# Attention and a gated convolutional network on one core: the same jobs issued in another order

## The chip, the core and the metric

The kernel runs on one core of a Trainium2 chip. The core's engines each work through a queue of their own, in order: TensorE (PE in the profile; PEld is its weight load), VectorE (DVE), ScalarE (ACT), GpSimd (POOL) and SyncE (SP), which here only issues DMAs. Engines wait for one another through semaphores. The metric is the device time of one execution in microseconds (us); the number quoted for a kernel is the median of its runs.

## What is computed

Attention over 8 batches of 8 heads, with rotary positions, and behind it a feed-forward stage whose gate is a causal convolution of five taps:

```python
q_rot, k_rot = rotate(q), rotate(k)                 # q, k, v: 8 x 8 x 576 x 64
scores = np.matmul(q_rot, k_rot.transpose(0, 1, 3, 2)) / np.sqrt(64)
attn = np.exp(scores - scores.max(-1, keepdims=True))
attn = attn / (attn.sum(-1, keepdims=True) + 1e-09)
x = np.matmul(attn, v)          # heads side by side: 8 x 576 x 512
gate_pre = sum(conv_w[k] * xp[:, k:k + S] for k in range(5))   # xp: x with 4 zeros ahead
gate = 1 / (1 + np.exp(-gate_pre))
out = (gate * (x @ w_val)) @ w_out                  # w_val, w_out: 512 x 512
```

## The kernel before

The 64 heads are worked on as 32 pairs, two heads side by side on the 128 partitions; four pairs make a batch. For one pair, in the order of the data:

- q and k are loaded (`load`, line 300 and 304) and multiplied by the cosine and the sine table (`rope_mul`, line 312: two instructions for a piece). Pair 0's products are added up on PE by `rope_mm` (line 327), by one product with the identity and one with `swap`, a signed exchange of halves that ACT writes at the start (`make_swap`, line 760); the sum is then cast by ACT (`qk_hi`, line 339). Later pairs add on DVE or GpSimd (`rope_add`, line 318). The tables arrive as two DMAs of 288 columns each; `tab_wrap` (line 763) copies 128 columns of the second to the table's end, and the warm-up of ACT's table stands behind the second one's issue. `k_wrap` (line 362) repeats the head of k behind its tail.
- `s_mm` (line 392) and `s_mix` (line 402) compute the scores into PSUM in nine tiles of 128 by 576; for each, `s_max` (line 428, DVE) scales the tile into SBUF and takes the row's bound, and `s_exp` (line 436, ACT) takes the exponential and its sum. Eight of them are tiles of one head (`p` in the profile) and the ninth holds the rest of both heads (`pm`).
- `t_mm` (line 412) transposes the exponentials on PE, `t_copy` (line 505 on ACT, 507 on DVE) takes them out of PSUM, and `pv_mm` and `pv_left` (lines 518 and 528) multiply them by v.
- `r_add` (line 536, GpSimd) adds the small constant to the nine sums, `r_inv` (line 545, DVE) takes the reciprocal, which is written into nine spare columns behind `pm`. So the last transpose of the pair, of `pm` with 73 columns ("64*73" in the profile and "73x64" in the order), needs the reciprocal of that pair. From there the sums go through DRAM to `x_norm` (line 577, DVE).
- `tap` (lines 603 to 610; two instructions on GpSimd), `x_hi` and `x_lo` (lines 584 and 591) prepare the network; `f_mm` (line 636) multiplies a batch by a weight, split in a high and a low half, in eight parts of six products for each pair of halves; `y_mul`, `y_hi`, `y_lo` (lines 649 to 664) come between the two weights, and `o_out`, `o_dma` (lines 677 and 681) write the result.

The weights and the taps arrive as 64-bit numbers, which arithmetic on their two halves turns into 32 bit in eight steps for each quarter of a weight (`weight_step`, lines 694 to 720) and six for the taps (`tap_step`).

The order is a table written out by hand of 3087 jobs, `ORDER` (line 38). `Plan.run` walks through it and issues each job to its engine; a letter behind a number picks the engine where there is a choice (V for DVE, A for ACT, G for GpSimd), `:n` picks the buffer, and `a<b` lets a job on PE wait for another. Jobs with two-input forms that DVE and GpSimd share (`PAIRED`, among them `rope_mul`, `rope_add`, `tap`, `x_lo`, `y_lo` and `weight_step`) wait, where they stand on GpSimd, for the last such job that stands before them on DVE. So the table sets the rows of every engine's queue. `FILLS` puts 20 products of no use on PE before one entry of the table, at the start. For pairs 0 to 6 (`WHOLE`, line 37) q and k are held in one piece; from pair 7 on they are split in a high and a low half, which triples the score products.

## Time and profile before

| what | us |
|---|---|
| runs of the kernel | 620.59, 621.61, 622.41 |
| median | 621.61 |
| profiled execution, its own time | 620.63 |
| span of the profiled execution | 618.8 |
| PE busy in the span | 609.4 (98%) |
| DVE busy | 526.8 (85%) |
| ACT busy | 472.9 (76%) |
| GpSimd (POOL) busy | 328.6 (53%) |

The span runs from the first instruction to the end of the last transfer; the execution's own time is 1.83 us longer. Busy time is the time in which at least one instruction of the engine is under way. Instructions of one engine overlap a little: the next one often starts 0.08 us before the end of the one ahead. PE's products are pipelined, and one that waits for its operand inside the pipeline still counts as busy, so a busy PE can hide waits.

### The profile page before, as it was taken

How to read it: one execution, taken by the hardware profiler on the slowest of the kernel's cores; microseconds unless marked ns; L12 is line 12 of the kernel's file. 1: busy time of each engine (PE TensorE's matmuls, PEld its weight loads, DVE VectorE, ACT ScalarE, POOL GpSimd, SP SyncE). 2: the span in 40 equal slices, each digit the busy share in tenths (PEclk: the TensorE clock that was granted, in tenths of full speed). 3: DMA queues.
4: the chain of work that ended last, by engine and by line, in shares of the span. 5: the costliest groups of instructions: out<-in, count | busy, mean ns of one | idle time of the engine just before them, and what ended most of it. 6: DMA issues, size and time to landing. Idle time of an engine off the chain costs nothing.

```text
span 618.8 us, 21223 instructions
## 1 busy us (share of the span) xinstructions
PE 609.4 (98%) x8797; PEld 511.8 (83%) x8797; DVE 526.8 (85%) x1091; ACT 472.9 (76%) x993; POOL 328.6 (53%) x306
## 2 busy tenths in 40 slices
PE   8899999999999999999999999999999999999997
PEld 7566679888897979879898889788888889889697
DVE  6999999999998899998888888989888888777653
ACT  4999999999878887788887788766768775767421
POOL 2366444635445656466455457564454654688441
PEclk9999999999999999999999999999999999999999
DMA  8564631543524341435343234342333524201202
GB/s 252 171 200 149 197 115 58 155 138 119 158 68 147 100 137 64 139 118 158 117 140 119 81 119 137 116 140 64 96 119 100 177 62 149 90 20 52 71 21 77
DMA packets 42722, 72.85 MB, mean 118 GB/s; under 512 B 15449, under 2 KB 18050, under 8 KB 42626
## 3 DMA queue, kind: packets, MB, share of 16 engines
q1 hardware_dynamic: 41938, 70.74, 36.3%
q8 instruction: 69, 1.13, 0.8%
q10 hardware_dynamic: 688, 0.75, 0.4%
q14 instruction: 27, 0.22, 0.1%
HBM read 61.89 MB, written 9.59 MB: 115 GB/s over the span
## 4 chain that ended last, share of the span: by engine, by line
PE 88%; DVE 6%; DMA 2%; ACT 2%; issue 1%; SPq 0%; DVEq 0%; POOL 0%; POOLq 0%
PE ps_f L636 34%; PE ps_a L518 18%; PE ps_s L392 16%; PE ps_t L412 11%; PE ps_s L402 4%; PE ps_a L528 3%; DVE p L428 3%; ACT p L436 1%; ACT pt L505 1%; PE ps_s L412 1%; DMA wst<-in_w_val 1%; DVE qin L312 1%; DMA rb<-rd 1%; DMA tab<-in_tab 1%; DVE pm L428 0%
## 5 line engine op out<-in xcount | busy, mean ns | idle before, releaser
L436 ACT ACTIVATE p<-p,nm 128x576 f32<-128x576 f32 x256 | 197.3, 773 | 33.3 <-DVE p L428 32.1
L428 DVE TENSOR_SCALAR_CACHE_REDUCE p<-ps_s 128x576 f32<-128x576 f32 x256 | 184.1, 752 | 24.3 <-PE ps_s L392 21.4
L505 ACT COPY pt<-ps_t 128x1024 f32<-128x1024 f32 (+1 forms) x138 | 126.0, 929 | 23.8 <-PE ps_t L412 22.3
L392 PE MATMUL ps_s<-k,q 64*128 64x288 f32 x1424 | 137.5, 316 | 1.6 <-DVE q L318 0.5
L518 PE MATMUL ps_a<-pt,v 128*64 128x320 f32 (+1 forms) x1024 | 133.2, 410 | 0.1
L392 PEld LDWEIGHTS ps_s<-k,q 64*128 64x128 f32 x1424 | 111.5, 185 | 17.6 <-issue 4.0
L636 PE MATMUL ps_f<-y,wout_hi 64*128 64x288 f32 (+2 forms) x1024 | 109.0, 298 | 0.0
L518 PEld LDWEIGHTS ps_a<-pt,v 128*64 128x64 f32 x1024 | 69.9, 137 | 47.1 <-DVE p L428 1.1
L606 DVE SCALAR_TENSOR_TENSOR g<-x,cw,g 128x576 f32<-128x576 f32 (+2 forms) x113 | 93.3, 828 | 7.1 <-POOL g L604 3.6
L412 PEld LDWEIGHTS ps_t<-ident,p 64*128 64x128 f32 x2172 | 86.1, 139 | 10.3 <-issue 2.2
L412 PE MATMUL ps_t<-ident,p 64*128 64x64 f32 x2172 | 92.2, 223 | 0.4
L636 PEld LDWEIGHTS ps_f<-y,wout_hi 64*128 64x128 f32 x1024 | 87.1, 186 | 0.6 <-DVE x L577 0.2
L636 PE MATMUL ps_f<-xh,wval_hi 64*128 64x288 f32 (+2 forms) x512 | 84.8, 303 | 0.0
L636 PE MATMUL ps_f<-xl,wval_hi 64*128 64x288 f32 (+2 forms) x512 | 82.0, 292 | 0.0
L636 PE MATMUL ps_f<-xh,wval_lo 64*128 64x288 f32 (+2 forms) x512 | 82.0, 292 | 0.0
L636 PE MATMUL ps_f<-y,wout_lo 64*128 64x288 f32 (+2 forms) x512 | 81.7, 292 | 0.0
L312 POOL TENSOR_TENSOR kin<-kin,tab 128x576 f32<-128x576 f32 x41 | 58.3, 1428 | 37.5 <-DVE q L352 12.5
L312 POOL TENSOR_TENSOR qin<-qin,tab 128x640 f32<-128x640 f32 x32 | 50.0, 1566 | 36.1 <-DVE g L606 10.4
L636 PEld LDWEIGHTS ps_f<-xh,wval_hi 64*128 64x128 f32 x512 | 54.6, 185 | 0.8 <-issue 0.5
L636 PEld LDWEIGHTS ps_f<-xl,wval_hi 64*128 64x128 f32 x512 | 54.6, 185 | 0.1
L636 PEld LDWEIGHTS ps_f<-xh,wval_lo 64*128 64x128 f32 x512 | 54.6, 184 | 0.0
L636 PEld LDWEIGHTS ps_f<-y,wout_lo 64*128 64x128 f32 x512 | 54.5, 185 | 0.0
(135 smaller groups left out, 924.9 us busy)
## 6 DMA issues: line engine op xcount, KB each, us to landing
kin<-in_k SPq DMA_DIRECT2D x31, 576.0 KB
qin<-in_q SPq DMA_DIRECT2D x31, 512.0 KB
v<-in_v SPq DMA_DIRECT2D x32, 320.0 KB
out_t<-o SPq DMA_DIRECT2D x28, 288.0 KB
rb<-rd SPq DMA_DIRECT2D x31, 144.0 KB
rb<-rd SPq DMA_DIRECT2D x31, 128.0 KB
wst<-in_w_val SPq DMA_DIRECT2D x4, 512.0 KB
o<-in_w_out SPq DMA_DIRECT2D x4, 512.0 KB
```

The source lines that it names most:

```text
L312: return eng.tensor_tensor(out=t[:, i, a:b], in0=t[:, 0 if p < RAW else i, a:b], in1=table[:, i, a:b], op=ALU.mult)
L392: T.matmul(out=tiles[h][:, half, 0:288], lhsT=operand(p, "q", h, x, c * 128, c * 128 + 128), rhs=operand(p, "k", h, y, k0 + half * 288, k0 ...
L402: inst = T.matmul(out=st["s8"][:, half], lhsT=operand(p, "q", h, x, 512, 640), rhs=operand(p, "k", h, y, D + half * 288, D + half * 288 + ...
L412: T.transpose(out=bank[0:src.shape[1], x, k * D:(k + 1) * D], in_=src[rows], identity=ident[rows, rows])
L428: return V.tensor_scalar(out=to, in0=st[f"s{i}"], scalar1=-SCALE if p in WHOLE else -1.0, scalar2=None, op0=ALU.mult, op1=ALU.min, accum_o ...
L436: return A.activation(out=to, in_=to if lifted else st[f"s{i}"], func=AF.Exp, bias=st[f"nm{i}"], scale=-1.0 if lifted else 1.0, accum_out= ...
L505: return A.copy(out=dst, in_=src)
L518: T.matmul(out=st[f"a{g}"][HEAD[h], 0:n], lhsT=st["v"][:, j, h, :], rhs=st[f"pt{g}"][:, h * 4 + j], start=(j == 0), stop=False)
L528: T.matmul(out=st[f"a{x}"][HEAD[h], 0:n], lhsT=st["v"][rows, 4, h, :], rhs=st["ptr"][rows, h, 0:n], start=False, stop=True)
L606: return eng.scalar_tensor_tensor(out=g, in0=x_sb, scalar=w, in1=g, op0=ALU.mult, op1=ALU.add)
L636: inst = T.matmul(out=acc[:, x, 0:hi - lo], lhsT=wt[w][HEAD[h], kc, dc * 128:(dc + 1) * 128], rhs=mv[HEAD[h], lo:hi], start=(turn == 0 and ...
```

## The change

The set of jobs, their code and the buffers' sizes stay as they are. Another table `ORDER` is put in: jobs stand in another order, some get another engine and other buffers. The fill products stand before entry 12 of the table and no longer before entry 14.

```diff
 ORDER = """
-7 22 11 8 16 0:0 10 31 9 27V 108 12V 28V 13V 29:0 17V 23V 24V 14:1 18V 30 99 32V 135 33V 25:2 15 144 1 19:3 2 3 26 4 109V 110V 34:0 111 20 21G 37:1
...
 """
-FILLS = {14: (20, 0)}
+FILLS = {12: (20, 0)}
```

What this does to the engines' queues is shown at three places.

The start on ACT, before. `tab` is the rotary table, `q_148` and `k_158` are pair 0's, `wst` is a quarter of a weight as it is loaded, and `ps_r` holds what PE has added up.

```order
L755 ACTIVATE warm<-x_81 128x1
L760 ACTIVATE swap<-ident 128x2x32 x2
L763 COPY tab<-tab 128x2x64
L339 COPY q_148<-ps_r 128x256
L339 COPY k_158<-ps_r 128x288
L339 COPY q_148<-ps_r 128x128
L339 COPY k_158<-ps_r 128x288
L694 ACTIVATE wst<-wst 128x512
L339 COPY q_148<-ps_r 128x256
L436 ACTIVATE p,sums_85<-p,nm 128x576 x7
```

And after:

```order
L755 ACTIVATE warm<-x_81 128x1
L763 COPY tab<-tab 128x2x64
L760 ACTIVATE swap<-ident 128x2x32 x2
L339 COPY q_136<-ps_r 128x128
L339 COPY q_136<-ps_r 128x256
L694 ACTIVATE wst<-wst 128x512
L339 COPY k_154<-ps_r 128x288 x2
L362 COPY k_154<-k_154 128x64
L718 CAST wval_hi<-wst 128x512
L339 COPY q_136<-ps_r 128x256
L436 ACTIVATE p,sums_85<-p,nm 128x576
```

The copy within the table has moved ahead of the two instructions that write `swap`. The first step of a weight stands ahead of both casts of k, and ACT takes the wrap of k and two casts of weights.

The start on DVE, before: the products of pair 0's q and k with the table, four steps on the taps (`o`, 20 columns), three on a weight, and the first score tiles (L428).

```order
L312 TENSOR_TENSOR qin_71<-qin_71,tab 128x128 x2
L312 TENSOR_TENSOR kin_69<-kin_69,tab 128x288
L312 TENSOR_TENSOR qin_71<-qin_71,tab 128x256 x2
L698 TENSOR_SCALAR o<-o 128x20
L707 TENSOR_SCALAR o<-o 128x20
L708 SCALAR_TENSOR_TENSOR o<-o 128x20
L712 TENSOR_SCALAR o<-o 128x20
L696 TENSOR_SCALAR wst<-wst 128x512
L702 TENSOR_SCALAR wst<-wst 128x512
L703 SCALAR_TENSOR_TENSOR wst<-wst 128x512
L428 TENSOR_SCALAR p,nm<-ps_s 128x576
L712 TENSOR_SCALAR wst<-wst 128x512
```

And after:

```order
L312 TENSOR_TENSOR qin_71<-qin_71,tab 128x128 x2
L312 TENSOR_TENSOR kin_69<-kin_69,tab 128x288 x2
L698 TENSOR_SCALAR o<-o 128x20
L707 TENSOR_SCALAR o<-o 128x20
L708 SCALAR_TENSOR_TENSOR o<-o 128x20
L712 TENSOR_SCALAR o<-o 128x20
L312 TENSOR_TENSOR kin_69<-kin_69,tab 128x288 x2
L312 TENSOR_TENSOR qin_71<-qin_71,tab 128x256 x2
L702 TENSOR_SCALAR wst<-wst 128x512
L703 SCALAR_TENSOR_TENSOR wst<-wst 128x512
L713 SCALAR_TENSOR_TENSOR o<-o 128x20
L712 TENSOR_SCALAR wst<-wst 128x512
```

The piece of q from column 256 to 384 has come to the front, two products of 256 columns have left DVE for GpSimd, where they are the first work, and the fifth step on the taps (L713, 20 columns) has come up from behind the first nine score tiles. Behind these rows there follow two more steps of weights, and then the first score tile.

PE around the last transposes of pair 6, before. `p` and `pm` are that pair's exponentials, `xh`, `xl` and `wval` belong to the first batch of the network, `k_1638` and `q_1723` to pair 7.

```order
L392 MATMUL ps_s<-k_1638,q_1723 128x288 x12
L412 MATMUL ps_t<-ident,p 128x64 x32
L412 MATMUL ps_t<-ident,pm 128x64 x8
L412 MATMUL ps_t<-ident,p 128x64 x4
L392 MATMUL ps_s<-k_1638,q_1723 128x288 x12
L412 MATMUL ps_t<-ident,pm 73x64 x2
L636 MATMUL ps_f<-xh,wval_hi 128x288 x2
L636 MATMUL ps_f<-xl,wval_hi 128x288 x2
```

And after:

```order
L392 MATMUL ps_s<-k_1708,q_1617 128x288 x12
L636 MATMUL ps_f<-xh,wval_hi 128x288 x2
L636 MATMUL ps_f<-xl,wval_hi 128x288 x2
L636 MATMUL ps_f<-xh,wval_lo 128x288 x2
L636 MATMUL ps_f<-xh,wval_hi 128x288 x2
L636 MATMUL ps_f<-xl,wval_hi 128x288 x2
L636 MATMUL ps_f<-xh,wval_lo 128x288 x2
L636 MATMUL ps_f<-xh,wval_hi 128x288 x2
L636 MATMUL ps_f<-xl,wval_hi 128x288 x2
L636 MATMUL ps_f<-xh,wval_lo 128x288 x2
L412 MATMUL ps_t<-ident,pm 128x64 x8
L412 MATMUL ps_t<-ident,pm 73x64 x2
```

Nine rows of the network's products, which are three parts of `f_mm`, now stand ahead of both transposes of `pm`; before, they stood behind them. The four transposes of `p` that stood ahead of the 73-column one now stand behind it.

## Rows read from the trace of the kernel before

**Rows 1.** The chain that ended last, by engine, from the profile page

```profile
PE 88%; DVE 6%; DMA 2%; ACT 2%; issue 1%; SPq 0%; DVEq 0%; POOL 0%; POOLq 0%
```

**Rows 2.** Busy time by stretch: all engines, granted clock and DMA; columns named first

```profile
core 0: us, PE busy (x) PEld busy (x) DVE busy (x) ACT busy (x) POOL busy (x), PEclk, DMA share, GB/s
0.00:4.28 4.28, 2.92 (x14) 2.92 (x15) 0.46 (x6) 1.78 (x4) 0.70 (x6) 1.00 0.57 165
4.28:11.26 6.98, 6.90 (x36) 5.03 (x34) 5.75 (x17) 1.71 (x5) 0.09 (x1) 1.00 0.87 267
11.26:40.00 28.74, 26.02 (x296) 18.65 (x298) 27.42 (x66) 26.35 (x57) 14.89 (x15) 1.00 0.63 205
40.00:80.00 40.00, 39.50 (x441) 26.25 (x439) 39.16 (x86) 39.55 (x90) 21.90 (x19) 1.00 0.52 164
80.00:117.17 37.17, 37.00 (x522) 30.14 (x522) 36.55 (x74) 34.94 (x72) 17.18 (x17) 1.00 0.38 119
...
160.00:560.00 400.00, 399.80 (x6065) 343.00 (x6060) 346.07 (x694) 307.23 (x641) 226.11 (x204) 1.00 0.36 113
```

**Rows 3.** Waits: PE from 120 to 600 us, then DVE from 20 to 117

```profile
PE ps_r L550 <- DVE sums L543: 0.5, 1, 0.5
...
DVE pm L428 <- PE ps_s L402: 0.5, 1, 0.5
DVE p L428 <- PE ps_s L392: 0.5, 2, 0.3
```

**Rows 4.** Timeline around pair 6's last transposes (DVE, PE): start, duration, operation

```profile
116.13 0.21 DVE L545 RECIPROCAL pm<-sums 128x9 f32<-128x9 f32 x1
...
117.17 0.22 PE L412 MATMUL ps_t<-ident,pm 64*73 64x64 f32 x2
...
117.69 0.29 PE L636 MATMUL ps_f<-xh,wval_hi 64*128 64x288 f32 x2
...
118.08 0.30 PE L636 MATMUL ps_f<-xh,wval_hi 64*128 64x288 f32 x2
```

**Rows 5.** Timeline of the start: ACT, then DVE, then PE

```profile
3.47 0.39 ACT L760 ACTIVATE swap<-ident 128x64 f32<-128x64 f32 x2
...
6.47 0.30 ACT L763 COPY tab<-tab 128x128 f32<-128x128 f32 x1 [2.62 <-DMA tab<-in_tab]
...
11.67 0.69 ACT L694 ACTIVATE wst<-wst 128x512 f32<-128x512 f32 x1 [2.04 <-DMA wst<-in_w_val]
...
9.40 0.43 DVE L696 TENSOR_SCALAR wst<-wst 128x512 f32<-128x512 f32 x1
...
11.26 0.76 DVE L428 TENSOR_SCALAR_CACHE_REDUCE p<-ps_s 128x576 f32<-128x576 f32 x1 [0.24 <-PE ps_s L392]
...
12.73 0.76 DVE L428 TENSOR_SCALAR_CACHE_REDUCE p<-ps_s 128x576 f32<-128x576 f32 x1 [0.36 <-PE ps_s L392]
...
5.57 0.70 PE L327 MATMUL ps_r<-qin,ident 128*128 128x256 f32 x2
...
9.99 1.25 PE L392 MATMUL ps_s<-k,q 64*128 64x288 f32 x8
```

**Rows 6.** Groups on DVE, 11.26 to 117.17 us: count, busy us, mean ns, idle before

```profile
L428 DVE TENSOR_SCALAR_CACHE_REDUCE p<-ps_s 128x576 f32<-128x576 f32 x58 | 41.2, 752 | 1.6 <-PE ps_s L392 1.1
...
L606 DVE SCALAR_TENSOR_TENSOR g<-x,cw,g 128x576 f32<-128x576 f32 x15 | 12.5, 831 | 0.2
...
L312 DVE TENSOR_TENSOR qin<-qin,tab 128x640 f32<-128x640 f32 x10 | 8.1, 823 | 0.0
...
L720 DVE TENSOR_TENSOR wval_lo<-wst 128x512 fp32r<-128x512 f32 x2 | 1.5, 758 | 0.0
```

**Rows 7.** Timeline: DVE operations beside a GpSimd one, and one alone

```profile
21.76 1.42 POOL L312 TENSOR_TENSOR kin<-kin,tab 128x576 f32<-128x576 f32 x1 [5.42 <-DVE kin L312]
...
22.22 0.99 DVE L713 SCALAR_TENSOR_TENSOR o<-o 128x20 f32<-128x20 uint32 x1
...
23.24 0.18 DVE L716 TENSOR_TENSOR cw<-o 128x20 f32<-128x20 f32 x1
```

More of the change, by code (lines that the diff above doesn't have):

```diff
@@ new lines @@
+631:1 632A:0 667G 668G 625:0 641A:0 633:3 634A:0 677:21 624 622 371 374V 334V 335V 336V 626<641 627:1 680:03 827G 337V 619 384A 583:3 406A 581 582
+669A 584 585 637:0 678:10 580 586 820G 604 828V 628 617 629 635:1 357:010 338 638A 682:23 636A 683:1 679 408:0 409 410 639:1 630 644 642 685:2 411
+645V 681 646A:0 676 647:0 648 692:23 829G 830G 831 898 684 695:20 693:33 412<646 413 414 821G 822G 415 416 643A 587G:0 640A 686 687:31 688:1 690:2
+358A 703:2 696 359V 360 823A 824V 704A:1 363A 361 364V 407V 705:0 706A:1 362 651:3 395A 396V 691 649 650 652 653 654 697:1 713V:1 833:20 694 709:3
@@ new lines @@
+1521A 1737:0 1787G 1789G 1790V 1522V 1739:1 1629G:0 1749:1 1692 1695:3 1750A:0 1791 1630V 1938V 2007 1696 2008V 1744 1693 1694 1697 1798:01 1490:2
+1939A 1698 1491 1801:22 1942 1799:33 1940G 1941G 1492 1493 1740 1738 1745 1746 1793:31 1796:1 1494<1746 1495 1496 1497 1802 1794:0 1760:0 1755 1800
+2009G 1699G:1 1700G:4 1334 1498 1720 1797 1758 1943G 1761A 1753:1 1751:3 1752V 1479:2 1480 1481 1482 1762A:0 2010V 1756A 1759A 1754A 1499V 1500V
+1808:01 1811:02 1944G 1795 1813:3 1483<1499 1484 1485 1829A:1 1809:13 1812 1486 1487 1945G 1488G 1489G 1814<1829 1815:1 1763:0 1803:10 1806:0 1701A:2
@@ new lines @@
+1962:12 1961 1842 2017G 1948 2018V 2019 2086 1969:1 1978A:0 1985A:0 1964:23 1965:1 1963 1553:0 1970<1985 1554 1555 1556 2082G 1843A:3 1773G:1 1542
+1966 1967:0 1968 1971:3 1972 1973 2083G 2026:23 1774V 1975:1 2027:22 1974 2084G 2307 2029:31 1976A:0 2028 2030 1557<1968 1558 1559 1560 1561V:0
+2021:21 1844G:0 2022:0 2023 1981:3 1982V 1979:0 1543:2 1544 1545 1988:3 1980A 2024:3 1986 2088V 1983 1984A 1546 1990A:0 1991:0 2031:10 2087V 2032:02
+2034:11 2089G 1989A 1775V 1987A 1547<1990 1548 1549 1550 2025 2041:3 2033 1776V 1551A:1 2085V 2036:10 2037:0 1862:2 1863 1864 2057A:1 2039:3 2090G
@@ new lines @@
+2832G 2297:0 2298 2299 2712 2281<2711 2282 2283 2284 2300 2729V:0 2756G 2823 2285A:0 2286 2895 2517G:4 2727:1 2728A 2717 2725:3 2726A:0 2723:2 2730
+2718 2732 2734A:0 2518G 2724V 2731A 2733A 2735:0 2301<2728 2302 2303 2304 2757A 2770:31 2590V 2628:2 2629 2305A:1 2630 2773:20 2774 2771:31 2631
+2617:0 2618 2619 2620 2519G 2591V 2736 2592V 2593V 2594 2765:13 2766:3 2768:2 2824G 2632<2592 2633 2772 2831G 2634 2635 2721:1 2621<2593 2636 2622
+2722A 2767 2637A 2780:32 2781:00 2769 2782 2833G 2834A 2623 2624 2793:1 2783:11 2449V 2737:3 2520V 2521V 2522 2450 2784 2835 2902 2794V:1 2825G 2826G
@@ new lines @@
+2739 2625 2740 2738 2741 2785:2 2595:1 2596 2801A:1 2786<2801 2742 2597 2598 2827A 2828G 2897V 2787:3 2788 2775:03 2776:2 2777 2797:2 2599<2788 2600
+2601 2602 2606:0 2626G 2607 2608 2609 2778:0 2779 2802:3 2798A 2603 2604A 2627G 2789 2790 2804 2896V 2805A 2795:1 2796A:1 2898V 2829V 2803V 2791:2
+2792A 2903V 2610<2805 2611 2612 2806V:1 2605V 2613 2799 2800A 2837:12 2614 2615A 2852:03 2840:01 2841 2855:13 2856 2853:22 2854 2904G 2905G 2906V
+2838:30 2839 2809:2 2810 2842:30 2811 2743G:2 2812 2813 2843:1 2844 2845:3 2846 2899G 2900G 2901G 2907 2929:1 2807:1 2808 2814 2847:30 2850:2 2851
@@ new lines @@
+3002 3003 3025:3 3026 3027 3028 3015<2980 3004 2973V 2974 3005 3008 3009G 3006A 3016 3017 3018 3029<2973 2994 2995V 2996V 3030 2678 3022 2982 3007V
+3019 3020A 3010G 3021G 3031 3039:2 3032 3033 3023G 3051:0 3052 3053 3054 3036 3037G 3040 3034A 3041 3042 3055<3037 3056 3075:1 3024G 3063:3 3064 3035V
+3065 3038G 3066 3057 3043<3038 3044 3045 3046 3047V:1 3048 3076 3077 3078 3058 3059V 3049V:0 3050 3061V 3062 3067<3047 3068 3069 3070 3079<3059 3060
+3071A 3072 3073V 3074 3080 3081 3082 3083A 3084 3085A 3086
```

219 lines of the change are left out of this document (98 added, 121 removed).

## The prediction

> **What bounds the kernel now.** I began with the chain that ended last. It gives PE 88% of the span [rows 1], and PE is busy nearly everywhere, so at first sight only PE's own work can matter. The table of stretches says otherwise for the first fifth [rows 2]. From 40 to 80 us PE is busy 39.50 of 40 us, but in that time it does 441 products, where from 160 to 560 us it does 6065 in 400 us, or 607 in 40. Its weight loads take 26.25 of 40 us in the one and 343.00 of 400 in the other. The mix of products differs, but not by that much: early on PE's products wait inside the pipeline. DVE shows for whom. From 11.26 to 117.17 us it is busy 27.42 + 39.16 + 36.55 = 103.1 of 105.9 us, and from 20 us on it waits three times, 1.0 us in all [rows 2, 3]. ACT is nearly as full from 40 to 80 us (39.55), less so on either side. From 160 us on DVE has 54 us to spare in 400 and PE is busy for 399.80; from 120 to 600 us PE has a single visible wait, of 0.5 us [rows 2, 3]. So there are two regimes: **DVE's queue until about 117 us, PE's work from there**.
>
> The Trainium skill says the same of such a profile: its page "Perfetto Trace Analysis", section "Identifying the Most-Contended Engine", calls the busy share of products no good measure and wants that of the weight loads read. The trace agrees: 26.25 of 40 us against 39.50 [rows 2]. By busy products alone no order could gain more than the few per cent that PE is idle, and the sum below would have no DVE term.
>
> The hand-over between the regimes can be placed. The last transpose of pair 6 takes 73 columns, since the reciprocals ride in it; it starts on PE at 117.17 us. The seventh reciprocal starts on DVE at 116.13 us, straight behind a score tile, in a queue that has hardly paused since 12.73 us [rows 4, 5]. I call that transpose the anchor. In this kernel the time is: when DVE's queue reaches the seventh reciprocal, plus the work that PE then still has. From pair 7 on the score products are three times as many, so that PE has more work for each DVE instruction and the other queues get ahead of it.
>
> **The change, part by part.** Only the table moves, so I count DVE's rows between the second score tile and the seventh reciprocal in both orders and price what differs. Two-input operations take 0.76 to 0.83 us by their groups, less 0.08 us by which the next one overlaps: 0.74 for 640 columns, 0.70 (between 0.68 and 0.75) for 512 or 576 [rows 6].
> - Gone from DVE up to there: two products of q with the table and three sums of q, 5 x 0.74 = 3.7; one correction of y and three subtractions or additions of weights, 4 x 0.70 = 2.8; a wrap of k, 0.1. Together 6.6 us.
> - New on it: a product and a sum of k, a low half of x and two additions of weights, 5 x 0.70 = 3.5; two taps, 2 x 0.75 = 1.5; one score tile more ahead of the reciprocal, 0.7; a weight's first step and two small copies, which have one input and fewer columns and which I price at half of 0.70 each, 1.0. Together 6.7 us. The two lists cancel.
> - Moved up to before the second score tile: the fifth step on the taps and two steps of a weight (L713 and L703). The two are 0.70 each. The taps' step is the odd one: it ran 0.99 us for 20 columns, ending just after a GpSimd product that began at 21.76 us for 1.42 us, while the next such step, alone, took 0.18 [rows 7]. In the new order it stands where GpSimd has its first products behind it. It leaves the stretch with 0.9 us whatever it takes there. Together 2.3 us less behind the second score tile.
>
> Here a rule of the Trainium skill bears: "SBUF — State Buffer", section "Terms", says that DVE and GpSimd arbitrate for a shared port pair and that the loser is blocked for the other's whole instruction. The 0.99 us step agrees. By it each two-input operation put on GpSimd can cost DVE time; by the count of DVE rows alone it cannot. This is the second rival below.
>
> **The start.** This is what the change pays. Before, `swap` was written at 3.47 us; now it stands behind the copy that waited for the second table until 6.47 us and took 0.30 us, so it is written from 6.74 to about 7.15 [rows 5]. DVE's first product now needs that same table. The first product with `swap` can thus start at about 7.2 us. Before, PE did its five sums of pair 0's q and k (256, 288, 128, 288 and 256 columns) from 5.57 us until the first score product at 9.99, which is 4.42 us for 1216 columns or 3.63 ns a column [rows 5]. Of the same five in the new order the second half of the first one (128 columns) and the four others (1088 columns) lie behind 7.2 us: 0.2 + 3.95 us, so PE is through at 11.4 us. ACT must cast both halves of k by then; it now stands before them at a weight's first step, whose quarter had landed by 9.40 us, when DVE took that step [rows 5]. The step's 0.69 us, two casts and the wrap are over at about 11.2. The first score tile followed the first score product by 11.26 - 9.99 = 1.27 us, which puts it at 12.6; with the L703 step between them the second comes 1.4 us later, at **14.0 us, against 12.73 before**. The bounds: 12.7 if the old pace is kept after all, 16 if ACT's casts come two microseconds late.
>
> **The sum at the reciprocal.** Before, 116.13 - 12.73 = 103.4 us from the second score tile. After: 14.0 + 103.4 - 2.3 + 0.1 = 115.2, or 0.9 us earlier.
>
> **PE behind the reciprocal.** Three parts of the network's product that stood behind the anchor stand ahead of it. A part took 0.39 us (117.69 to 118.08 [rows 4]): 1.2 us of PE's work is done while PE waits anyway. Four short transposes move the other way, about 0.1 us. So 1.1 us less is left. If DVE did not bind, this part is worth nothing, as the products are merely exchanged: from 0 to -1.2 us.
>
> **Behind the anchor, and what I cost at nothing.** Later moves lie beside PE work: between 160 and 560 us DVE, ACT and GpSimd are busy 346, 307 and 226 of 400 us [rows 2]. The new order takes some jobs from ACT and gives DVE and GpSimd a few per cent more, which that spare time hides. If the cover is gone at one place, the row of such a wait is 0.5 us [rows 3]; I allow 1 us either way. The last outputs go to ACT and not DVE, one copy for one copy. The fill products keep their number. PE pauses between them and 7.2 us, where before it had the sums to do; the granted clock was 1.00 (the 2.4 GHz level) in all stretches [rows 2], also in the first with PE busy 2.92 of 4.28 us, so I cost that at nothing.
>
> Total: -0.9 - 1.1 = -2.0 us. Against the profiled execution of 620.63 that is 618.6. The median of the runs, 621.61, is 0.98 above it, so **619.6** is the median that I predict.
>
> **The rivals.**
> - *No change: the start eats it.* It decides on ACT. The casts of k are the last step before the scores as soon as the weight's quarter lands after about 9.6 us; DMAs are at 0.87 of their share in that stretch, and another quarter landed at 11.67 us [rows 2, 5]. If the one ACT waits for lands two microseconds after 9.40, the second score tile is at 16: +2.0, so 621.6. For it: ACT now blocks on a landing that DVE used to take. Against it: the loads are issued in the same order.
> - *Slower: GpSimd blocks DVE.* Up to the seventh addition of sums (L536) GpSimd has 37 two-input operations instead of 32, and of the long ones of 640 columns 11 instead of 4. A DVE operation that begins in the shadow of one loses up to 0.8 us (0.99 - 0.18 [rows 7]). In the DVE regime each such loss reaches the end. Three more of them eat the gain (3 x 0.7 = 2.1); six more give +4.2 - 2.0 = +2.2, ten +5, so 624 to 627, of which I take 624.5. For it: five more at 1.42 us [rows 7] are 7 us, 13% of the 54 us that GpSimd was busy there [rows 2]. Against it: it was idle for half of the stretch, and DVE's groups show little beyond the alone-time (823 and 831 ns for long ones against 752 for a tile [rows 6]).
> - *More gain.* If the start keeps its old pace (12.7: -1.3 more) and DVE's three waits of 1.0 us go too [rows 3], the sum is -4.3, so 617.3. For it: the counts on DVE even out with what it did while waiting. Against it: `swap` cannot be earlier than the second table.
> - *Another engine holds the anchor.* ACT was as full as DVE from 40 to 80 us [rows 2]. Then DVE's 0.9 us is worth nothing and the three parts of products still count: 620.5, within the first rival's bounds.
>
> **How the numbers follow.** A measurement of this kernel tells about 0.3%, or 1.9 us, from no change, so "faster" begins at 619.7, just above my forecast. The forecast itself (618.6 to 620.8, from the bounds of the start and of the later stretch) has 42 in 100, of which a little over half lies below 619.7. More gain has 20, no change with the ACT case 20, GpSimd's blocking 18. So faster 0.24 + 0.20 = 0.44, same 0.18 + 0.20 = 0.38, slower 0.18. The range runs from the "more gain" case to the first third of the slower one: 617.0 to 622.8.
>
> **What would show it.** The second score tile on DVE at about 14 us; `swap` at about 6.8; the seventh reciprocal at about 115.2 and the 73-column transpose close behind it; PE's end 2 us earlier, and the part between the anchor and PE's end shorter by 1.1 us. The taps' 20-column step short. The prediction is wrong if the reciprocal comes later than 116.1; then either the second score tile is at 16 (ACT), or DVE's groups at L312, L318 and L606 have grown in their mean (GpSimd). It is wrong in its frame if the time changes behind the anchor by more than 1 us.

## Result and the profile after

The changed kernel is **slower**, by 0.8%: a median of 626.45 us (624.68 to 626.99) against 621.29 us for the kernel before, a ratio of 1.008 with a 95% interval of 1.0064 to 1.0096. Its profiled execution took 624.68 us with a span of 622.9 us, 4.05 us over the profiled execution of before; it is the fastest of six, the others took 626.05 to 626.99 us.

The table of stretches of the kernel after, with the columns of [rows 2] (us, then busy time and count for PE, PEld, DVE, ACT and POOL, the granted clock, DMA):

```profile
4.28:11.26 6.98, 5.60 (x27) 4.43 (x26) 4.44 (x14) 2.56 (x8) 1.45 (x2) 1.00 0.86 282
11.26:40.00 28.74, 26.96 (x305) 20.22 (x303) 28.04 (x69) 26.40 (x59) 17.01 (x18) 1.00 0.66 205
40.00:80.00 40.00, 39.79 (x453) 27.43 (x453) 38.73 (x87) 39.15 (x86) 21.68 (x19) 1.00 0.47 146
80.00:117.17 37.17, 36.88 (x514) 29.79 (x512) 36.19 (x70) 33.92 (x71) 18.57 (x17) 1.00 0.43 136
160.00:560.00 400.00, 397.53 (x6018) 340.31 (x6016) 354.60 (x700) 298.88 (x628) 235.67 (x207) 1.00 0.36 111
```

In the first stretch PE does 27 products where it did 36: that is the start. Up to 80 us it catches up (296 + 441 products before, 305 + 453 now). Between 160 and 560 us it does 6018 products where it did 6065, and is idle for 2.5 us where it was idle for 0.2 [rows 2]. So the loss lies mostly **behind** 160 us, where I had costed the change at nothing. At the same time DVE is busy for 354.60 us there and not 346.07, GpSimd for 235.67 and not 226.11.

The start, as in [rows 5], and the reciprocal of pair 6, as in [rows 4] (timeline: start, duration, engine, operation, idle time before and what ended it):

```profile
6.64 0.40 ACT L760 ACTIVATE swap<-ident 128x64 f32<-128x64 f32 x2
7.27 0.46 PE L327 MATMUL ps_r<-qin,ident 128*128 128x128 f32 x2 [1.38 <-issue]
11.69 4.69 PE L392 MATMUL ps_s<-k,q 64*128 64x288 f32 x24
...
11.39 0.17 DVE L713 SCALAR_TENSOR_TENSOR o<-o 128x20 f32<-128x20 uint32 x1
13.00 0.76 DVE L428 TENSOR_SCALAR_CACHE_REDUCE p<-ps_s 128x576 f32<-128x576 f32 x1
14.38 0.75 DVE L428 TENSOR_SCALAR_CACHE_REDUCE p<-ps_s 128x576 f32<-128x576 f32 x1
...
117.27 0.21 DVE L545 RECIPROCAL pm<-sums 128x9 f32<-128x9 f32 x1
```

`swap` is written from 6.64 us, PE's first sum starts at 7.27 after a pause of 1.38 us, the first score product at 11.69, and the second score tile at 14.38 us. The taps' fifth step, 0.99 us before [rows 7], takes 0.17. The seventh reciprocal comes at 117.27 us, where I had 115.2 and the kernel before 116.13.

PE's waits from 120 to 610 us (engine, line, what it waited for: us in total, times, longest), against the single one of 0.5 us in [rows 3]:

```profile
PE ps_s L392 <- DVE p L428: 1.7, 1, 1.7
PE ps_r L550 <- DVE sums L543: 1.2, 1, 1.2
PE ps_f L636 <- DVE xl L591: 0.6, 1, 0.6
PE ps_r L550 <- DVE pt L507: 0.5, 1, 0.5
PE ps_t L412 <- DVE x L577: 0.3, 1, 0.3
```

The first is at 265 us. This is DVE, then GpSimd, then PE of the kernel after around it:

```profile
259.24 0.81 DVE L312 TENSOR_TENSOR qin<-qin,tab 128x640 f32<-128x640 f32 x1
260.16 1.10 DVE L318 TENSOR_TENSOR qin<-qin 128x640 f32<-128x640 f32 x1
261.29 1.60 DVE L345 TENSOR_SCALAR q<-qin 128x640 fp32r<-128x640 f32 x1
262.93 1.91 DVE L352 SCALAR_TENSOR_TENSOR q<-qin,q 128x640 fp32r<-128x640 f32 x1
264.76 0.75 DVE L428 TENSOR_SCALAR_CACHE_REDUCE p<-ps_s 128x576 f32<-128x576 f32 x1
...
258.68 1.91 POOL L603 TENSOR_SCALAR term<-x,cw 128x576 f32<-128x576 f32 x1
260.67 1.87 POOL L604 TENSOR_TENSOR g<-term,g 128x576 f32<-128x576 f32 x1
262.50 1.66 POOL L664 TENSOR_TENSOR y<-g,y 128x576 fp32r<-128x576 f32 x1
...
265.57 1.06 PE L392 MATMUL ps_s<-k,q 64*128 64x288 f32 x11 [1.67 <-DVE p L428]
```

DVE's sum, cast and low half of pair 16's q take 1.10, 1.60 and 1.91 us. L318 ends at 261.26, L345 at 262.89 and L352 at 264.84 us, 0.67, 0.35 and 0.68 us after a GpSimd instruction that lay beside it (260.59, 262.54 and 264.16 us), which is about what each takes alone (0.82 and 0.49 us, and 0.82 for the third) less its overlap. GpSimd's scaling by a tap (L603) takes 1.91 us, too. The two engines hold each other in turn, and the score tile for whose buffer PE waits starts at 264.76 us.

The change itself made this meeting: of the jobs at this place it moved one of the two products of pair 16's q from GpSimd to DVE, the cast of that q from ACT to DVE, and the tap (12, 2) from DVE to GpSimd, right beside them. In the kernel before GpSimd has little to do here, and the low half of q takes 0.82 us (DVE, then GpSimd, which has only the first of these two instructions between 261.3 and 264.3 us):

```profile
262.68 0.82 DVE L352 SCALAR_TENSOR_TENSOR q<-qin,q 128x640 fp32r<-128x640 f32 x1
...
261.28 0.66 POOL L342 CAST k<-kin 128x576 fp32r<-128x576 f32 x1
264.33 0.75 POOL L603 TENSOR_SCALAR term<-x,cw 128x576 f32<-128x576 f32 x1 [2.39 <-DVE g L606]
```

The last row also shows the scaling by a tap with no DVE operation holding it: 0.75 us, against 1.91.

A measure that does not depend on one wait: adding up, for every product that PE has begun, the spacing that products of its kind have when they follow each other undisturbed (an estimate from all of PE's rows), PE of the kernel after stands 0.55 us ahead of the kernel before just ahead of this place, 2.1 us behind after it, 2.1 us behind at 560 us and 3.8 us behind at its last product. So the place takes 2.6 us from PE and the last 50 us take 1.7. A held operation need not cost PE anything: between 270 and 560 us DVE's operations are longer than the shortest tenth of their kind by 6.1 us in sum before and by 7.6 us after (an estimate, too, from all of DVE's rows), and PE is 2.1 us behind at both ends. Where an experiment below keeps PE's order, I compare it directly, by the start of the 73-column transposes of pairs 13 and 15, which lie on either side of the place, and of PE's last product:

| kernel | pair 13 | pair 15 | from 13 to 15 | last product |
|---|---|---|---|---|
| after | 246.60 | 283.34 | 36.74 | 618.39 |
| tap_v | 246.49 | 285.75 | 39.26 | 620.89 |
| q_later | 247.64 | 284.08 | 36.44 | 619.09 |
| place | 247.90 | 284.44 | 36.54 | 619.20 |
| tail | 246.38 | 283.16 | 36.78 | 617.52 |
| clean | 246.51 | 283.03 | 36.52 | 617.13 |
| clean2 | 247.97 | 284.17 | 36.20 | 618.53 |
| short | 247.91 | 282.59 | 34.68 | 617.56 |
| fills | 246.49 | 283.96 | 37.47 | 618.83 |
| all3 | 246.45 | 281.12 | 34.67 | 615.64 |

### The profile page after: what moved, and what is told of

Its sections match the earlier page's. It is cut to its first block, busy times and chain, and to the rows that moved or that the text cites. A ratio compares the mean times of both kernels' runs of the same rounds, so it can differ in the third digit from the quotient of the medians.

```text
span 622.9 us, 21236 instructions
## 1 busy us (share of the span) xinstructions
PE 608.8 (98%) x8797; PEld 513.0 (82%) x8797; DVE 536.6 (86%) x1098; ACT 464.3 (75%) x977; POOL 343.2 (55%) x318
## 5 line engine op out<-in xcount | busy, mean ns | idle before, releaser
L428 DVE TENSOR_SCALAR_CACHE_REDUCE p<-ps_s 128x576 f32<-128x576 f32 x256 | 183.8, 752 | 25.1 <-PE ps_s L392 22.1
L505 ACT COPY pt<-ps_t 128x1024 f32<-128x1024 f32 (+1 forms) x131 | 120.2, 934 | 25.8 <-PE ps_t L412 24.9
L518 PE MATMUL ps_a<-pt,v 128*64 128x256 f32 (+1 forms) x1024 | 131.9, 409 | 0.2
L636 PE MATMUL ps_f<-y,wout_hi 64*128 64x288 f32 (+2 forms) x1024 | 107.0, 296 | 0.0
L606 DVE SCALAR_TENSOR_TENSOR g<-x,cw,g 128x576 f32<-128x576 f32 (+2 forms) x110 | 92.8, 850 | 10.1 <-POOL g L604 7.2
L412 PEld LDWEIGHTS ps_t<-ident,p 64*128 64x128 f32 x2172 | 83.6, 139 | 12.6 <-issue 3.9
L412 PE MATMUL ps_t<-ident,p 64*128 64x64 f32 x2172 | 90.6, 224 | 0.8 <-DVE p L428 0.4
L636 PEld LDWEIGHTS ps_f<-y,wout_hi 64*128 64x128 f32 x1024 | 84.9, 185 | 0.4
L312 POOL TENSOR_TENSOR qin<-qin,tab 128x640 f32<-128x640 f32 (+1 forms) x39 | 59.3, 1528 | 41.4 <-DVE g L606 19.3
L636 PE MATMUL ps_f<-y,wout_lo 64*128 64x288 f32 (+2 forms) x512 | 79.4, 292 | 0.0
L312 POOL TENSOR_TENSOR kin<-kin,tab 128x576 f32<-128x576 f32 x36 | 51.2, 1428 | 36.0 <-DVE q L352 16.0
L636 PEld LDWEIGHTS ps_f<-y,wout_lo 64*128 64x128 f32 x512 | 52.2, 185 | 0.0
```

Source lines behind the costliest of these rows:

```text
L312: return eng.tensor_tensor(out=t[:, i, a:b], in0=t[:, 0 if p < RAW else i, a:b], in1=table[:, i, a:b], op=ALU.mult)
L412: T.transpose(out=bank[0:src.shape[1], x, k * D:(k + 1) * D], in_=src[rows], identity=ident[rows, rows])
L428: return V.tensor_scalar(out=to, in0=st[f"s{i}"], scalar1=-SCALE if p in WHOLE else -1.0, scalar2=None, op0=ALU.mult, op1=ALU.min, accum_o ...
L505: return A.copy(out=dst, in_=src)
L518: T.matmul(out=st[f"a{g}"][HEAD[h], 0:n], lhsT=st["v"][:, j, h, :], rhs=st[f"pt{g}"][:, h * 4 + j], start=(j == 0), stop=False)
L606: return eng.scalar_tensor_tensor(out=g, in0=x_sb, scalar=w, in1=g, op0=ALU.mult, op1=ALU.add)
```

## Experiments

**Theory 1**: the loss comes from places behind 117 us where DVE and GpSimd hold each other and PE stands right behind; the largest is at 260 us, two smaller ones are in the last 50 us. **Theory 2**: DVE has too much to do there, however it is arranged. **Theory 3**: the loss is that of the start and of DVE's queue up to 117 us. All medians with the ratio to the kernel before measured beside them, whose own median lay between 620.85 and 621.68 us; a difference between two rows, or to the 626.45 us of the kernel after, can be off by some tenths:

| kernel | median us | ratio (95% interval) |
|---|---|---|
| tap_v | 628.21 | 1.0106 (1.0091 to 1.0121) |
| q_later | 624.53 | 1.0050 (1.0033 to 1.0067) |
| tail | 624.14 | 1.0050 (1.0031 to 1.0070) |
| both | 627.15 | 1.0093 (1.0078 to 1.0108) |
| place | 625.28 | 1.0062 (1.0047 to 1.0076) |
| clean | 624.14 | 1.0053 (1.0038 to 1.0068) |
| clean2 | 624.07 | 1.0049 (1.0037 to 1.0062) |
| short | 622.36 | 1.0028 (1.0016 to 1.0040) |
| fills | 625.48 | 1.0070 (1.0057 to 1.0082) |
| all3 | 621.87 | 1.0008 (0.9999 to 1.0017) |
| tiles_early | 624.78 | 1.0057 (1.0044 to 1.0071) |
| tiles_late | 624.37 | 1.0049 (1.0036 to 1.0062) |
| qlo_late | 624.19 | 1.0059 (1.0043 to 1.0076) |
| parts | 624.11 | 1.0043 (1.0028 to 1.0059) |
| parts2 | 621.26 | 1.0001 (0.9992 to 1.0010) |

Of the order's long lines the diffs show only the words around an edit. There 1259 is the tap (12, 2), 1574 and 1575 are the cast and the low half of pair 16's q, 1573 its sum, 1422, 1424, 1427 and 1429 are pair 15's score tiles, 1373 and 1374 the addition and the reciprocal of pair 14's sums. Line numbers in the traces of tap_v, q_later, tail and both lie 4 higher.

**tap_v**, one job from GpSimd to DVE:

```diff
-1571G 1259G 1320
+1571G 1320
...
-1422:30 1423
+1422:30 1259V 1423
```

> The changed kernel with one job moved: the tap (12, 2), two instructions on GpSimd (L603 and L604, 258.7 to 262.5 us in the changed kernel's trace), goes to DVE and stands behind the two score tiles of pair 15. Theory 1, blocking behind the hand-over: DVE's sum, cast and low half of q (L318, L345, L352 at 260.16, 261.29 and 262.93, which took 1.10, 1.60 and 1.91 us) are no longer held by GpSimd, the score tile starts by about 262.5 instead of 264.76, and the wait of PE's scores (1.7 us at 265.57) goes. The time falls by 1.7 to 2.7 us, to about 624. Theory 2, too much DVE work there: DVE has one operation more, nothing is gained, 626 to 627. Theory 3, all of the loss lies in the first fifth: no change behind 117 us, 626 to 627.

It came out the other way, 628.21 us. GpSimd went on to its next work, the low half of y (L664, here L668), and that met DVE instead (DVE, then GpSimd):

```profile
259.16 2.04 DVE L316 TENSOR_TENSOR qin<-qin,tab 128x640 f32<-128x640 f32 x1
263.03 1.91 DVE L356 SCALAR_TENSOR_TENSOR q<-qin,q 128x640 fp32r<-128x640 f32 x1
264.86 0.74 DVE L432 TENSOR_SCALAR_CACHE_REDUCE p<-ps_s 128x576 f32<-128x576 f32 x1
...
258.56 1.96 POOL L668 TENSOR_TENSOR y<-g,y 128x576 fp32r<-128x576 f32 x1
262.74 1.52 POOL L668 TENSOR_TENSOR y<-g,y 128x576 fp32r<-128x576 f32 x1
```

The rotation of q (L316) takes 2.04 us instead of 0.81 and the low half of q again 1.91; the score tile stands at 264.86, not earlier. Behind PE's wait the granted clock now falls, which the profiled execution of the kernel after had been spared (1.00 throughout). The stretches of tap_v, columns as above:

```profile
264.00:266.00 2.00, 0.33 (x4) 0.33 (x6) 2.00 (x4) 0.35 (x1) 2.00 (x3) 1.00 0.04 9
266.00:268.00 2.00, 1.00 (x13) 0.63 (x9) 2.00 (x5) 1.31 (x5) 2.00 (x2) 1.00 0.76 212
268.00:270.00 2.00, 1.74 (x36) 1.74 (x38) 1.60 (x6) 0.98 (x2) 1.92 (x2) 0.64 0.28 83
270.00:272.00 2.00, 2.00 (x26) 2.00 (x24) 1.26 (x3) 1.52 (x3) 1.61 (x2) 0.51 0.00 0
```

PE was busy for 1.33 of 4 us from 264 us on, and then the clock is at 0.64 and 0.51 in the two stretches up to 272 us; the record has the lower of its two levels, 0.50 (1.2 GHz), from 268.55 to 271.96 us. So a wait at this place can cost PE twice. **both**, the same edit with those of tail, went the same way, to 627.15 us:

> The changed kernel with the edits of tap_v and tail together. Theory 1: the two gains add up, 3.5 to 5 us less, 621.4 to 623, about the kernel before or 0.5 us under it by the profile, since up to 230 us the changed kernel's PE stood 0.5 us ahead. Theory 3: 626 to 627.

**q_later**, DVE's order alone:

```diff
-1573V 1574V 1575 1149A
+1573V 1149A
...
-1422:30 1423
+1422:30 1574V 1575 1423
```

> The changed kernel with the cast and the low half of pair 16's q (L345, L352) moved on DVE behind the two score tiles of pair 15 that stood behind them; GpSimd's queue is as it was. Theory 1, blocking that matters because PE has no slack at these tiles: the tiles start at about 261.3 instead of 264.76, PE's wait goes, 1.7 to 2.7 us less, about 624, though the two operations may still be held by GpSimd later. Theory 2, the blocked time itself counts wherever it falls: no gain, 626 to 627.

**place**, the same two jobs further back and the sums of pair 14 ahead on GpSimd:

```diff
-1117G 1373 1378A
+1373 1117G 1378A
...
-1573V 1574V 1575 1149A
+1573V 1149A
...
-1427:3 1383
+1427:3 1574V 1575 1383
```

> The changed kernel with three jobs of its place at 260 us moved: the cast and the low half of pair 16's q (L345, L352) stand on DVE behind four score tiles, the reciprocal and the normalization that stood behind them, and GpSimd's addition to pair 14's sums (L536) stands ahead of the low half of y. Against the run with the cast and low half moved behind two tiles only (624.5), in which PE still waited for that reciprocal. Theory 1, blocking that counts only where PE stands right behind: PE's waits at 264 to 268 us go altogether, 2.5 to 3 us under the changed kernel's 626.45, 623.3 to 624. Theory 2, DVE's lost time counts wherever it falls: 624.5 or more, since it still loses some beside GpSimd.

The medians, 624.53 and 625.28 us, seem to bear out theory 1. The traces don't: from pair 13 to pair 15 PE took 36.44 and 36.54 us, only 0.2 to 0.3 us less than in the kernel after. In both the wait for the score tile is gone, but another has come for it. What the medians gain over that these traces don't assign; the mean granted clock of q_later's executions was 0.999 to 1.000, while that of the kernel after was 0.995 in three of six. Moving DVE's jobs within its queue is worth little, as theory 2 has it; the next run decides between the two.

**short**, GpSimd's work cut and DVE's queue as it was:

```diff
 def tap(p, k, a, b, eng=V):
     st = state[p]
     c = p % PPB
+    b = a + 8 if (p, k) == (12, 2) else b
...
 def y_lo(b, dc, lo, hi, eng):
+    if (b, dc) in ((2, 0), (2, 1)): return G.memset(y_part(b, 1)[:, dc, lo:hi].bitcast(F32), 0.0)
```

> The changed kernel, DVE's queue as it is, with GpSimd's work at 260 us cut: the tap (12, 2) is done for 8 of 576 columns, and the low halves of y of the pairs 8 and 9 are filled with zeros (both leave out a part of the computation). If GpSimd's instructions hold DVE's sum, cast and low half of q: L318, L345 and L352 fall to about 0.82, 0.49 and 0.82 us, the next score tile starts at about 262.4 instead of 264.76, PE's wait of 1.7 us goes, and with it the fall of the granted clock behind it: 2 to 2.7 us less, 623.8 to 624.5. If the five DVE operations in a row are the cause and their length is their own: 626 to 627.

DVE in short (this execution began 1.3 us later than the one above):

```profile
260.58 0.81 DVE L312 TENSOR_TENSOR qin<-qin,tab 128x640 f32<-128x640 f32 x1
261.50 0.82 DVE L318 TENSOR_TENSOR qin<-qin 128x640 f32<-128x640 f32 x1
262.36 0.89 DVE L345 TENSOR_SCALAR q<-qin 128x640 fp32r<-128x640 f32 x1
263.28 0.83 DVE L352 SCALAR_TENSOR_TENSOR q<-qin,q 128x640 fp32r<-128x640 f32 x1
264.02 0.75 DVE L428 TENSOR_SCALAR_CACHE_REDUCE p<-ps_s 128x576 f32<-128x576 f32 x1
```

The three operations behind the rotation take 0.82, 0.89 and 0.83 us, PE's wait of 1.7 us is gone, and from pair 13 to pair 15 PE takes 34.68 us: **2.06 us less** than in the kernel after, with DVE's operations, their number and their order unchanged. So it is GpSimd that lengthens them, and theory 2, by which their length is their own, falls; all3 below, which started as early as the kernel after, repeats it (34.67 us). The median is 622.36, 4.1 us less, more than I expected; the kernel after's own median lies 1.8 us over its profiled execution, and those 1.8 us, late starts and a lowered clock as shown under fills, are mostly missing here, too: three executions lie at 622.21 to 622.36 us, two at 623.85 and 624.20. The cut takes GpSimd work away, so it shows the cause and is no remedy.

**tail**, three jobs of the last 50 us:

```diff
-2820G 2821G 2748V
+2820G 2748V
...
-2925:1 2883:2
+2925:1 2821V 2883:2
...
-2887G:3 2888G:4
+2887G:3 2888V:4
...
-2749V 2750 2893V 2744V:0
+2749V 2744V:0 2750 2893V
```

> The changed kernel with three jobs changed in its last 50 us: the tap (29, 4) goes from GpSimd to DVE behind the next score tile, the low half of x of pair 30 from GpSimd to DVE, and the low half of x of pair 28 stands on DVE ahead of a tap that waits for GpSimd. Theory 1: the two small additions of sums (L542, 1.38 us each at 573.43 and 582.57, of which 0.2 is their own) are no longer held by GpSimd and PE's waits for them (1.2 and 0.5 us, L550) and for the low half of x (0.6 us, L636) go; 1.5 to 2.3 us less, about 624.4. Theory 3, all of the loss lies in the first fifth: 626 to 627.

In the kernel after (GpSimd, then DVE) the second small addition of sums is held by a tap's addition:

```profile
573.37 1.41 POOL L604 TENSOR_TENSOR g<-term,g 128x576 f32<-128x576 f32 x1
...
572.99 0.33 DVE L542 TENSOR_SCALAR sums<-sums 128x2 f32<-128x2 f32 x1
573.43 1.38 DVE L542 TENSOR_SCALAR sums<-sums 128x2 f32<-128x2 f32 x1
```

0.33 us for the one and 1.38 us for the other, both on 2 columns. The changed kernel has a second such row at 582.57 us (1.38 us); the kernel before has one (1.36 us at 576.10 us). With the edit PE's last product starts at 617.52 and not 618.39 us: 0.9 us, half of what I expected, since PE still waits twice there (0.8 us for an exponential, 0.4 us for GpSimd's low half of x). The median, 2.3 us lower, holds besides fewer of the late starts and lowered clocks shown under fills (623.77 to 626.11 us in four executions).

**clean** (place and tail together) and **clean2** (tail; the cast of q on ACT, the addition of sums and pair 16's rotation ahead, the tap on DVE behind the tiles; the low half of q stayed on DVE, as that job has no other engine):

> The changed kernel with the edits of the run before (place) and of the run tail. Theory 1: the two gains, 2.7 and 2 us, add up: 621.3 to 622.3, within 0.1% of the kernel before, with PE about 0.5 us ahead of it up to 230 us and no granted clock under 1.00 behind. Theory 3, the loss sits in the start and in DVE's queue up to 117 us: 624 or more.

> The changed kernel with its tail as in the run tail and the place at 260 us taken apart: the cast of pair 16's q goes from DVE to ACT, its low half from DVE to GpSimd, the tap (12, 2) from GpSimd to DVE behind pair 15's tiles, and the addition to pair 14's sums ahead on GpSimd. By theory 1 nothing on DVE is held there and neither PE's wait nor a lower granted clock follows: 3.7 to 4.7 us under the changed kernel, 621.5 to 622.5; PE's lead of 0.5 us over the kernel before, held up to 230 us, should be left at 240 us. If the wait only moves on, as in the run clean: 624.

Both missed, at 624.14 and 624.07 us. The wait only moved on, 36.52 and 36.20 us from pair 13 to 15. The text of clean2 had that as its other case; that of clean had 624 or more for theory 3, and its trace puts the loss at the place all the same. In clean it stands at a copy behind the low half of q; in clean2 the tap that went to DVE met GpSimd's rotation there and took 1.53 us. Three arrangements of the same jobs at this place give back 0.2 to 0.5 us of some 2.1.

**fills**, one number:

```diff
-FILLS = {12: (20, 0)}
+FILLS = {12: (26, 0)}
```

> The changed kernel with 26 fill products instead of 20 at its start, so that PE has work until about 7.2 us and does not pause between 5.9 and 7.2 us. If that pause lowers PE's clock in some executions: the products of 256 columns at 8 to 10 us take 0.6 us and never 1.06, the executions that start 1.1 to 1.2 us late go, and the median falls by 0.5 to 1 us, to 625.5 to 626. If the late starts come from DMAs that land late: no change, 626.5.

The median fell by 1.0 us, to 625.48. Five of the nine profiled executions with the changed start and 20 fill products began 1.0 to 1.4 us later than that of the kernel after. Two of them, q_later and short (PE's first sums, from the timeline), a stretch of short with its clock, and the same product in fills:

```profile
7.21 0.77 PE L331 MATMUL ps_r<-qin,ident 128*128 128x128 f32 x2 [1.32 <-issue]
8.20 1.06 PE L331 MATMUL ps_r<-qin,ident 128*128 128x256 f32 x2
...
8.39 1.06 PE L327 MATMUL ps_r<-qin,swap 128*128 128x256 f32 x2
8.00:10.00 2.00, 2.00 (x6) 1.59 (x5) 1.83 (x7) 0.65 (x3) 0.00 (x0) 0.50 0.95 279
...
8.14 0.59 PE L327 MATMUL ps_r<-qin,swap 128*128 128x256 f32 x2
```

After the pause the products of 256 columns take 1.06 us, in fills 0.59. In short the granted clock is 0.50 at that time (0.50 from 7.81 to 11.22 us, 1.00 from 4.40 us until then). In q_later the stretch from 8 to 10 us is printed with 1.00, but its trace holds no record of the clock before 10.08 us, and the pace of the products shows the lower level from PE's first product on: the fill products ahead of the pause are 0.213 us apart, where they are 0.109 apart in the kernel before from 5.0 us on, when its record begins. It is the same in both, place and clean2, whose records begin at 10.52 to 10.56 us. So in four of the five the clock had not yet risen when PE paused, and only in short had it risen and fell again; in the kernel after it rose at 5.91 us, as the last fill product ended. With work for PE until 7.2 us none of this occurs in the trace of fills, and no execution of it, nor of all3, shows the spread of the kernel after (fills 625.10 to 625.92, all3 621.64 to 622.11). The 1.0 us of the medians is less firm than the traces: by the ratios above it is 0.6 us, with intervals that overlap, and it is a net figure, since all executions of fills have a mean granted clock of 0.995 to 0.997 (the fall that follows) and only three of six of the kernel after have. In fills the wait at 265 us is still there, and the clock falls behind it:

```profile
264.00:266.00 2.00, 0.55 (x8) 0.55 (x10) 2.00 (x6) 0.57 (x1) 1.76 (x4) 0.98 0.00 0
266.00:268.00 2.00, 2.00 (x31) 1.83 (x30) 1.88 (x7) 1.29 (x5) 2.00 (x3) 0.50 0.86 246
268.00:270.00 2.00, 2.00 (x38) 2.00 (x38) 1.62 (x5) 1.50 (x2) 2.00 (x2) 0.67 0.19 49
```

That costs 0.73 us from pair 13 to 15 (37.47 against 36.74).

**all3**, the edits of fills, tail and short together:

> The changed kernel with the 26 fill products, the edits of the run tail, and GpSimd's work at 260 us cut as in the run short (the tap (12, 2) for 8 of 576 columns, the low halves of y of the pairs 8 and 9 filled with zeros: a part of the computation is left out). If the three places hold all of the loss: 620.3 to 621.3, level with the kernel before or 0.5 us under it, as PE's lead up to 220 us had it, with PE's lead at 240 us still there. If something else costs time: 622 or more.

621.87 us, 4.6 us under the kernel after and 0.6 over the kernel before, with an interval that just holds no change. PE's last product starts at 615.64 us, 2.75 us before that of the kernel after. The difference of the medians can be made up so, as an estimate: 2.1 us the place at 260 us (by the table), 0.7 the tail (2.75 less 2.07), 1.0 the pause at the start (fills), and 0.8 is what is left of 4.6; the fall of the clock behind the place, which cost 0.73 us in fills, is about as large, but that it is the rest was not tested. The last 0.6 us against the kernel before (in the traces PE's last product starts 1.0 us later, at 615.64 against 614.61) stays without a cause of its own: of the 2.6 us at the place short gave back 2.06, of the 1.7 us in the tail the edit of tail gave back 0.9, and PE still waits 0.8 and 0.4 us in the tail of all3. all3 leaves out a part of the computation, so it is no better version of the kernel, and no edit that computes everything came below the kernel before.

**tiles_early and tiles_late**, the kernel before with four score tiles done twice:

```diff
 def s_max(p, i, t, part):
...
+    if p in (1, 2, 3, 4) and i == 2: V.tensor_scalar(out=to, in0=st[f"s{i}"], ...)
     return V.tensor_scalar(out=to, in0=st[f"s{i}"], ...)
```

(18 to 21 for tiles_late).

> The kernel before, with one score tile of each of the pairs 1 to 4 put into SBUF twice (L428, 0.68 us from start to start each, 2.7 us of added DVE work between 20 and 90 us). If DVE's queue sets the time up to 117 us, as the prediction has it: 2.7 us more, 624.4. If PE's work sets it there already: no change, 621.7. If half of the stretch is ACT's: about 1.3 more.

> The kernel before, with the same four extra tiles in the pairs 18 to 21 (about 300 to 400 us). By the prediction's frame DVE's spare time there hides them: 621.7, at most 0.3 more. If the order leaves no slack at single places even there, as it did at 260 us in the changed kernel: up to 2.7 more.

3.4 and 3.0 us for 2.7 us of DVE work. In the traces PE is 3.8 us late from pair 4 on in the one, and 3.1 from pair 22 on in the other, and no later part of the kernel gives anything back. A part of the 3.8 is the start: the first 73-column transpose of that execution is 0.2 us late already. The first agrees with the prediction's frame, the second does not.

**qlo_late**, the same with another operation:

```diff
 if n == "q":
+    if p in (18, 19, 20, 21): V.scalar_tensor_tensor(out=lo, ...)
     return V.scalar_tensor_tensor(out=lo, ...)
```

> The kernel before, with the low half of q (L352, 0.74 us from start to start) of the pairs 18 to 21 computed twice, 3.0 us of added DVE work at about 280 to 380 us. If DVE's idle time there hides what is not on the chain of score tiles: at most 0.5 us more, 621.3 to 621.8. If any work put in front of DVE's next score tile delays PE there, as the extra tiles did: 2 to 3 us more, 623.3 to 624.3.

3.3 us for 3.0 us of work, though nothing that is computed waits for the extra operation but what stands behind it on DVE. The stretch from 280 to 380 us, of qlo_late, and then of before:

```profile
280.00:380.00 100.00, 98.12 (x1484) 84.45 (x1482) 86.01 (x178) 79.30 (x167) 51.76 (x43) 1.00 0.39 120
```

```profile
280.00:380.00 100.00, 99.88 (x1534) 87.38 (x1534) 85.81 (x182) 81.91 (x172) 55.05 (x45) 1.00 0.41 125
```

In the kernel before DVE is idle for 14.2 of 100 us there. With 3 us more to do it is busy for 86.01 and not 85.81 us: the added work did not go into the idle time, it pushed everything back (1484 products of PE in place of 1534).

**parts and parts2**, the kernel before with the three parts of `f_mm` (408, 409, 410) moved alone, ahead of both transposes (639) or ahead of the 73-column one (644):

```diff
-681 639:0
+681 408:1 409 410 639:0
```

```diff
-682:32 644
+682:32 408:1 409 410 644
```

> The kernel before with one part of the change alone: three parts of the network's product (L636, 1.2 us of PE work) stand ahead of both last transposes of pair 6 and no longer behind them. By the prediction's step, PE waits there for DVE anyway and the work is done for nothing: 1.1 us less, 620.3. If PE's products are merely exchanged: no change, 621.4. In the changed kernel PE's lead grew by about 0.5 us at this place, so 0.5 less would fit as well.

> The kernel before with the three parts of the network's product (1.2 us of PE work) moved right ahead of the 73-column transpose of pair 6, behind the scores of pair 7, where PE waits for the reciprocal. Prediction's step: 1.1 us less, 620.2. If the parts delay the transpose, since PE waits there for less than their 1.2 us: between no change and 1 us more.

Where the prediction put it, the part gains nothing: 1.0001 (0.9992 to 1.0010). Further ahead it costs 2.9 us, because its PSUM buffer is still in use there; PE in parts:

```profile
117.40 0.40 PE L636 MATMUL ps_f<-xh,wval_hi 64*128 64x288 f32 x2 [1.52 <-ACT pt L505]
119.92 0.22 PE L412 MATMUL ps_t<-ident,pm 64*73 64x64 f32 x2
```

## Why the prediction was wrong

**What bounds the kernel now.** The reading that DVE's queue sets the time in the first fifth agrees with tiles_early, but that run doesn't prove it, since the same work costs as much at 300 us. The reading that PE's work alone sets it behind does not hold: a DVE operation added there costs its whole length, as one at 50 us does (tiles_late, qlo_late). Of DVE's idle time, 54 us in 400 [rows 2], 17.2 us is waiting for the scores of its next tile, the largest share (the rest goes to other products of PE and to GpSimd and ACT), and PE in turn gets its next buffers from DVE. My account, which fits these runs but was not tested further, is that an operation put in front of a tile delays this ring of waits, and that PE, which has no idle time of its own, never catches up.

**"Behind the anchor, and what I cost at nothing" is the step that failed.** I took busy shares of 346, 307 and 226 of 400 us for cover and allowed 1 us either way. The runs put 2.1 us at one place (short), 0.7 to 0.9 in the tail (tail, all3) and, in executions in which the granted clock falls behind the place, another 0.7 there (fills). At the anchor itself nothing was lost: the 73-column transpose starts at 117.75 and not 117.17 us with 1.2 us more of PE's work done, so PE is 0.6 us ahead there, and the whole loss came behind it.

**The slower rival had the mechanism and its price, but not its place.** GpSimd does block DVE: at one place, from the start of the rotation (L312) to the next score tile, 264.76 - 259.24 = 5.5 us became 264.02 - 260.58 = 3.4 us in short, three losses of 0.7 us on the mean, the price that I had put on one. I counted such meetings up to 117 us only; there they cost little: DVE's means are 844 ns for L606 and 834 for L312, against 831 and 823 [rows 6]:

```profile
L606 DVE SCALAR_TENSOR_TENSOR g<-x,cw,g 128x576 f32<-128x576 f32 x16 | 13.4, 844 | 0.2
L312 DVE TENSOR_TENSOR qin<-qin,tab 128x640 f32<-128x640 f32 x8 | 6.4, 834 | 0.0
```

The operations held at 260 us are of two kinds: some with two inputs, and a cast with one (L345, 0.49 us alone, 1.60 here); in the tail it is a small addition with one input (L542). The Trainium skill, page "SBUF — State Buffer", section "SBUF: two separate sides", says that DVE shares a pair of ports with GpSimd when it has two inputs in SBUF or runs in a two-port mode, that whoever starts first holds it for its whole instruction, and that the other is blocked. The traces agree: each of the three held operations at 260 us ends 0.35 to 0.68 us after a GpSimd instruction has, the small addition 0.03 us after one, and with GpSimd's tap cut and zeros written in place of its subtraction the three at 260 us take 0.82, 0.89 and 0.83 us (short). The same skill's page "Perfetto Trace Analysis", section "Optimizing Scalar/DVE Operations", warns that moving work between DVE and GpSimd might not help for that reason; tap_v shows that here, 1.8 us slower for one such move.

**The start.** The second score tile came at 14.38 us, 0.4 later than worked out, so the sum of sums and casts was right. What I costed at nothing, PE's pause before 7.2 us, was the error: it costs some executions 1.0 to 1.4 us and the median 0.6 to 1.0 (fills). The clock of 1.00 in the first stretch of before [rows 2] was misread: the trace holds no record of it ahead of 5.00 us, and until then PE's fill products are 0.213 us apart, half the pace of 0.109 that they have behind it. So PE starts at the lower level (1.2 GHz) in every trace here, and what counts is when the clock rises. Where PE did not pause it rose at 6.8 to 7.1 us at the latest (tiles_early, parts and parts2, whose first 73-column transpose is 0.2 to 0.4 us late); behind the pause of the changed kernel it rose as late as 10.1 to 10.6 us.

**The sum at the reciprocal.** -0.9 us was forecast, +1.1 came (117.27 against 116.13). The start gives 0.4 of the 2.1 us between. The work that I counted away did go: the operations between the second tile and the reciprocal add up to 2.1 us less (from all rows of both traces), against 2.2 forecast. But the stretch became only 0.5 us shorter (102.89 against 103.40), because idle time between operations grew by 0.6 us and fewer of them overlap their predecessor. What made them overlap less I did not test. The prediction named two causes for a reciprocal that comes late, ACT at the start (the second tile at 16 us) and longer groups on DVE, and neither is seen: the second tile came at 14.38 us, and the groups' means grew by 13 and 11 ns.

**The three parts of products**, priced at -1.1 us, are worth 0.0 in the kernel before (parts2). My own rows said so: the reciprocal is done at 116.34 and the transpose starts at 117.17 us [rows 4], behind the twelve score products that stand ahead of it in PE's queue. PE did not wait for the reciprocal there.

**The numbers.** Of the range, 617.0 to 622.8, the upper end was drawn through the first third of the slower rival, whose own value, 624.5, was nearer to the result than the forecast. It had 18 in 100. That the result lies within that rival's 624 to 627 us is luck, since its count of meetings ended at 117 us.
